# Linear attention and two MLPs: raw weights begun earlier on ScalarE, v loads moved to GpSimd, k's small exponential as its own step

## The chip, the cores and the metric

The kernel runs on one core of a Trainium2 chip. The metric is device time in microseconds (us), the median of several executions; smaller is better. The engines are TensorE (PE; its weight loads are shown as PEld), VectorE (DVE), ScalarE (ACT), GpSimd (POOL) and SyncE (SP, which only issues transfers). An engine works off its own instructions in the order of the program.

## The reference

```python
# q, k, v: (8, 8, 576, 64); q scaled by 8, k by 3.682
q_s = softmax(q, axis=-1); k_s = softmax(k, axis=2)       # over the features; over the sequence
kv = einsum('bhsd,bhse->bhde', k_s, v)
x = einsum('bhsd,bhde->bhse', q_s, kv)                    # -> (4608, 512)
g = x @ w_gate; val = x @ w_val                           # (512, 1536) each
x = (g * sigmoid(g) * val) @ w_out                        # (1536, 512)
h = maximum(maximum(x @ w1, x @ w2), x @ w3)              # (512, 768) each
return h @ w_out2                                         # (768, 512)
```

## The kernel before

The 4608 tokens are nine blocks of 512 (`BLOCKS`): three alone, then three pairs, worked off as six stages. Every fp32 product is made as three products of split factors (`...h` and `...l` are the high and the low part), each a run of six matmuls of 128x512. The pair stages use a scheme with seven products for eight; its unit uses four banks of PSUM (`b0` to `b3`) in turn, and `wino_copy` (L891), `wino_add` (L901), `consume` (L857 is the Silu, L866 the multiply) empty them on ScalarE and VectorE. `wino_hi` (L764) and `wino_lo` (L768) make split weights for it.

Nothing reorders the program afterwards: each engine runs its instructions in the order in which the code issues them. That order has three sources. First the loads, by the table `LOADS`. Then `PROLOGUE`, a table written by hand: each entry is one step, and the program's function `run` issues it. The steps that matter here:

- `load_v` is `first_load_v` (L278): six transfers for each half hf of block 0's v, hf 0 begun by ScalarE, hf 1 by GpSimd. The memsets of `kvhi` and `kvlo` (L2648) stand ahead of all loads on GpSimd.
- `act` is `conv_act` (L602): the raw weights lie as 64-bit numbers; ScalarE makes the upper word (L612) and the lower (L616) into two parts, `dve` is `conv_dve` (L628), which joins them on VectorE and also begins the store and further loads; `hi` (L646) and `lo` (L649) split the joined weight. `act 0` and `act 1` read the first two 512-KB pieces of w_gate, `act 2` the first of w_val.
- `k_exp` (L338, L342) and `q_exp` (L358) are exponentials, `q_sum` and `q_mul` the division of q's softmax, `kv` (L258) the product of k and v on TensorE, `scale` (L406) its division, `qt` (L381) transposes of q, `take` (L388) their copies to SBUF, `x` (L392) the block's x in a bank, `xh` (L484) and `xl` (L487) the two parts of x; `mm` a first product of x and a weight group (L798).
- `silu` (L2611) loads the Silu table ahead of its use.

The index behind a step's name is the half (0 or 1) of block 0 with its four heads, called block 0 and block 1 below and in the steps.

From then on a planner walks through the stages' units and puts work into each engine's gaps by estimated durations; its table of steps for the softmax of k is `k_steps`, a chain for each run (j, hf): j is the token block, hf the half of the heads. There `B` is a step for VectorE or GpSimd, `X` one on ScalarE that counts table loads, `A` one on ScalarE. `k_sub` subtracts k's maximum from the large part (part 0, L195) and the small (part 1, L200), `k_exp` (L206) exponentiates them. Exponentials and the Silu use different tables, so a change between them costs a table load on ScalarE.

The lines the change touches:

Of the kernel before, what the change touches and what calls it, by code (L numbers as in the profile page):

```python
# [11 lines left out]
F32 = mybir.dt.float32  # L12
# [9 lines left out]
def linear_attention_moe_moe_kernel(  # L22
# [170 lines left out]
    def k_sub(t, c, part, eng):  # L193
        if part == 0:
            eng.tensor_tensor(  # L195
                out=t["k"], in0=t["k"],
                in1=c["kb"].unsqueeze(2).to_broadcast([128, HH, R, D]), op=ALU.subtract,
            )
        else:
            eng.tensor_tensor(  # L200
                out=t["kr"][0:SR], in0=t["kr"][0:SR], in1=c["kb"][0:SR], op=ALU.subtract
            )

    def k_exp(t, c, part):
        a = t["kr"][0:SR] if part else t["k"]
        nc.scalar.activation(out=a, in_=a, func=AF.Exp)  # L206
# [69 lines left out]
        )  # L276

    def first_load_v(t, hf):  # L278
        eng = (nc.scalar, nc.gpsimd)[hf]
        for g in range(HP):  # L280
            h0 = hf * HH + 2 * g
            for u in range(2):
                eng.dma_start(
                    out=t["v"][:, 0:R, g, u, 0:D],
                    in_=v[0, h0 + u, 0:SM, :].rearrange("(p r) d -> p r d", r=R),
                )
            eng.dma_start(
                out=t["v"][0:SR, R, g, :, 0:D],
                in_=v[0, h0:h0 + 2, SM:S, :].rearrange("h p d -> p h d"),
            )  # L290
# [932 lines left out]
    def k_steps(runs, n_buf):  # L1223

        steps = []
        loads = [k_loads(kbuf[n % n_buf], *run) for n, run in enumerate(runs)]

        def load(n, part):
            if n < len(runs):
                steps.append(("load", 1.8 if n == 0 else 1.0, ((n, part), loads[n][2:] if part else loads[n][:2])))  # L1230

        load(0, 0)
        load(0, 1)
        for n, (j, hf) in enumerate(runs):
            c, t = {}, kbuf[n % n_buf]
            if j in LATER:
                steps.append(("gate", 0.0, ("later", j)))
            if n_buf == 2:
                load(n + 1, 0)
            steps.append(("loaded", 0.0, (n, 0)))  # L1240
            steps.append(("D=", 1.15, lambda i, c=c, t=t: k_max(t, c, i)))
            steps.append(("loaded", 0.0, (n, 1)))
            steps += [("D", 0.42, lambda c=c, t=t: k_max_rest(t, c)), ("G", 1.4, lambda c=c: k_max_all(c))]
            steps += [("B", (1.22, 0.42)[i], lambda e, c=c, t=t, i=i: k_sub(t, c, i, e)) for i in range(2)]
            steps.append((("X", 1), 1.5, lambda c=c, t=t: (k_exp(t, c, 0), k_exp(t, c, 1))))

            def kv(bank, c=c, t=t):
                for g in range(HP):
                    kv_mm(t, c, g, bank)

            steps += [("wait", KV_WAIT, None), ("P", 1.25, kv)]
            steps += [("D", 1.1, lambda c=c, t=t: kv_scale(t, c)), ("bank", 0.0, None)]
            if n_buf == 1:
                load(n + 1, 0)
            load(n + 1, 1)
            steps += [("gate", 0.0, ("x", j - 2, hf))] * (j > 2) + [
                ("A", 0.6, lambda c=c, j=j, hf=hf: kv_hi(c, j, hf)),
                ("D", 0.4, lambda c=c, j=j, hf=hf: kv_lo(c, j, hf)),
            ]
            steps.append(("open", 0.0, ("kv", j, hf)))  # L1260
        return steps
# [1314 lines left out]
    with tc.manual_schedule():  # L2576
# [17 lines left out]
        def run(name, i, g=None):  # L2594
            t = first[i] if i in (0, 1) else None
            if name == "act":
                conv_act(i, False, i)
            elif name == "dve":
                conv_dve(i, False)
                store_plain(*conv[i])  # L2600
                load_more(i)
            elif name == "hi":
                kind, f = conv[i]
                group_hi(kind, f, (0, kind, f // 2, 0, f % 2), 2 * i)
            elif name == "lo":
                kind, f = conv[i]
                group_lo(kind, f, 2 * i)
            elif name == "load":
                loads(i)
            elif name == "silu":  # L2610
                nc.scalar.activation(out=tops[0], in_=minus_i[:, 0:HP], func=AF.Silu)  # L2611
            elif name == "mm":
                kind, f = conv[i]
                product(("b0", "b2")[i], (0, kind, f // 2, 0, f % 2, 0), "b11", True, True, False)
            elif name.startswith("load_"):
                {"k": first_load_k, "q": first_load_q, "v": first_load_v}[name[5:]](t, i)
            elif name == "xh":
                x_hi(c[i]["px", g], 0, i * HP + g)
            elif name == "xl":
                x_lo(c[i]["px", g], 0, i * HP + g)  # L2620
            else:
                FIRST[name](t, c[i], g)
# [20 lines left out]
        for _ in range(EARLY):  # L2643
            nc.tensor.matmul(
                out=early, lhsT=first[0]["kv"][:, 0], rhs=first[0]["kv"].rearrange("p g n -> p (g n)"), start=True, stop=True
            )
        for a in (*kvhi, *kvlo):
            nc.gpsimd.memset(a.bitcast(F32), 0.0)  # L2648
        for step in LOADS:
            run(*step)  # L2650
        for step in PROLOGUE:
# [9 lines left out]


LOADS = (
    ("load_k", 0), ("load_q", 0), ("load_k", 1), ("load_v", 0), ("load", 1), ("load_q", 1),
    ("load_v", 1), ("load", 6),
)
EARLY = 5
PROLOGUE = (
    ("km", 0), ("plain", 0, 0), ("turn", 0), ("plain", 0, 1), ("top", 0), ("q_max", 0), ("minus", 0, 0),
    ("minus", 0, 1), ("plain", 0, 2), ("minus", 0, 2), ("k_exp", 0, 0), ("k_exp", 0, 1), ("k_exp", 0, 2), ("q_sub", 0),  # L2670
    ("plain", 1, 0), ("plain", 1, 1), ("km", 1), ("q_exp", 0, 0), ("q_exp", 0, 1), ("kv", 0, 0), ("kv", 0, 1),
    ("turn", 1), ("plain", 1, 2), ("q_sum", 0), ("q_mul", 0, 0), ("q_mul", 0, 1), ("qt", 0, 0), ("take", 0, 0),
    ("qt", 0, 1), ("take", 0, 1), ("act", 0), ("scale", 0), ("x", 0, 0), ("x", 0, 1), ("top", 1),
    ("minus", 1, 0), ("minus", 1, 1), ("minus", 1, 2), ("q_max", 1), ("xh", 0, 0), ("xh", 0, 1), ("q_sub", 1), ("k_exp", 1, 0),
    ("k_exp", 1, 1), ("k_exp", 1, 2), ("dve", 0), ("xl", 0, 0), ("xl", 0, 1), ("hi", 0), ("q_exp", 1, 0), ("q_exp", 1, 1),
    ("lo", 0), ("kv", 1, 0), ("kv", 1, 1), ("q_sum", 1), ("act", 1), ("mm", 0), ("silu", 0), ("q_mul", 1, 0), ("q_mul", 1, 1),
    ("scale", 1), ("qt", 1, 0), ("take", 1, 0), ("qt", 1, 1), ("take", 1, 1), ("x", 1, 0), ("x", 1, 1), ("dve", 1), ("hi", 1),
    ("lo", 1), ("act", 2), ("mm", 1), ("xh", 1, 0), ("xh", 1, 1), ("dve", 2), ("hi", 2), ("xl", 1, 0), ("xl", 1, 1), ("lo", 2),
    ("act", 3), ("dve", 3), ("hi", 3), ("lo", 3), ("act", 4), ("act", 5), ("dve", 4), ("dve", 5),
)  # L2680

# [31 lines left out]
```

## Time and profile before

| | us |
|---|---|
| median of 3 runs | 1452.77 (1451.65 to 1453.37) |
| profiled execution | 1452.13, its span 1450.4 |
| PE busy | 1439.6 (99% of the span) |
| DVE busy | 1031.6 (71%) |
| ACT busy | 711.1 (49%) |
| POOL busy | 160.4 (11%) |

The span is the profiled part of an execution; 1.7 us lie around it. A row of the timeline gives start, duration, engine, line, operation, the tiles written and read, and in brackets how long the engine was idle before and what ended that. "xN" is a count of instructions.

### The profile page before, as it was taken

To read this page: it belongs to the slowest core of one execution; us is meant where nothing else is said; L and a number is where in the kernel's file an instruction comes from. 1 tells how busy PE (TensorE), PEld (TensorE's weight loads), DVE (VectorE), ACT (ScalarE), POOL (GpSimd) and SP (SyncE) were. 2 spreads that over 40 slices of the span, in tenths; PEclk is the share of its full clock that TensorE was granted. 3 is DMA by queue.
4 is the path that set the end of the run, shared out by engine and by line. 5 is a ranking of instruction groups with operands and counts; after the bars stand their busy time and mean duration, and the time that the engine had idled before them with its cause. 6 is when DMAs were issued, how large, how long until landed. Compare 5 with 4: busy or idle time off the path is not lost.

```text
span 1450.4 us, 20587 instructions
## 1 busy us (share of the span) xinstructions
PE 1439.6 (99%) x6880; PEld 1178.6 (81%) x6880; DVE 1031.6 (71%) x1815; ACT 711.1 (49%) x1198; POOL 160.4 (11%) x282
## 2 busy tenths in 40 slices
PE   9999999999999999999999999999999999999998
PEld 6887888888888888878878888888888888888887
DVE  7888766968786777788878767667876655577433
ACT  6988654544564435454644463335343532254222
POOL 3111111111222321221021100000000000000000
PEclk9999999999999999999999999999999999999999
DMA  9989588794988898986787587774766676646664
GB/s 273 343 282 363 192 254 245 224 330 142 292 295 299 306 346 290 282 259 197 223 268 241 195 270 229 203 211 153 231 193 199 210 214 195 187 163 223 207 197 155
DMA packets 268456, 347.42 MB, mean 240 GB/s; under 512 B 126304, under 2 KB 152672, under 8 KB 268352
## 3 DMA queue, kind: packets, MB, share of 16 engines
q1 hardware_dynamic: 241904, 263.79, 59.9%
q0 software_dynamic: 23904, 81.61, 14.8%
q8 instruction: 55, 0.90, 0.3%
q10 hardware_dynamic: 2544, 0.72, 0.2%
q14 instruction: 49, 0.40, 0.1%
HBM read 255.59 MB, written 90.44 MB: 239 GB/s over the span
## 4 chain that ended last, share of the span: by engine, by line
PE 93%; DVE 4%; DMA 2%; issue 1%; ACT 1%; SPq 0%; POOL 0%; DVEq 0%; ACTq 0%; POOLq 0%
PE pb L798 61%; PE pacc L819 13%; PE pacc L831 6%; PE pb L831 5%; PE pb L819 3%; PE pkv L258 1%; PE pacc L811 1%; PE px L456 1%; PE px L457 1%; PE px L458 1%; DVE tall L901 1%; DMA twos<-sums_W 1%; PE pacc L798 0%; DMA k_sb<-in_k_dram 0%; DVE wall L768 0%
## 5 line engine op out<-in xcount | busy, mean ns | idle before, releaser
L798 PE MATMUL pb<-t,wall 128*128 128x512 f32 x1116 | 273.5, 390 | 2.0 <-DVE tall L901 2.0
L798 PE MATMUL pb<-b11h,wall 128*128 128x512 f32 x752 | 263.4, 391 | 0.2 <-DVE tall L866 0.2
L798 PE MATMUL pb<-b21h,wall 128*128 128x512 f32 x752 | 262.0, 390 | 0.0
L798 PEld LDWEIGHTS pb<-t,wall 128*128 128x128 f32 x1116 | 208.8, 188 | 47.4 <-issue 1.7
L901 DVE TENSOR_TENSOR tall<-tall,pb 128x512 f32<-128x512 f32 x188 | 128.6, 686 | 125.8 <-PE pb L798 107.3
L798 PEld LDWEIGHTS pb<-b11h,wall 128*128 128x128 f32 x752 | 141.1, 188 | 30.8 <-DVE tall L866 0.6
L798 PEld LDWEIGHTS pb<-b21h,wall 128*128 128x128 f32 x752 | 141.2, 188 | 29.5
L798 PE MATMUL pb<-b21l,wall 128*128 128x512 f32 x376 | 146.6, 390 | 0.7 <-DVE b21l L2028 0.4
L798 PE MATMUL pb<-b11l,wall 128*128 128x512 f32 x376 | 146.5, 390 | 0.0
L891 ACT COPY tall<-pb 128x512 f32<-128x512 f32 x124 | 72.6, 588 | 125.0 <-PE pb L798 118.1
L649 DVE TENSOR_TENSOR wall<-plain,wall 128x512 fp32r<-128x512 f32 x126 | 86.0, 689 | 28.2 <-ACT wall L646 28.0
L646 ACT CAST wall<-plain 128x512 fp32r<-128x512 f32 x126 | 76.0, 617 | 29.5 <-DMA plain<-raw_W 7.3
L866 DVE TENSOR_TENSOR tall<-s,pb 128x512 f32<-128x512 f32 x81 | 55.3, 684 | 47.6 <-PE pb L798 47.4
L819 PE MATMUL pacc<-ow,hhi 128*128 128x512 f32 x288 | 89.1, 390 | 0.0
L819 PE MATMUL pacc<-hhi,ow 128*128 128x512 f32 x264 | 87.8, 395 | 0.0
L798 PE MATMUL pb<-t1h,wall 128*128 128x512 f32 x248 | 86.5, 389 | 0.3 <-DVE tall L901 0.3
L798 PE MATMUL pb<-b22h,wall 128*128 128x512 f32 x248 | 86.6, 390 | 0.0
L798 PEld LDWEIGHTS pb<-b21l,wall 128*128 128x128 f32 x376 | 70.6, 188 | 16.0 <-DVE b21l L2028 0.8
L831 PE MATMUL pacc<-hhi,ow 128*128 128x512 f32 x248 | 82.5, 390 | 0.0
L798 PEld LDWEIGHTS pb<-b11l,wall 128*128 128x128 f32 x376 | 70.6, 188 | 14.1 <-issue 0.2
L831 PE MATMUL pb<-hhi,ow 128*128 128x512 f32 x216 | 68.0, 389 | 0.0
L2002 ACT COPY pb<-pb 128x512 f32<-128x512 f32 x42 | 24.0, 570 | 86.7 <-PE pb L798 86.7
(313 smaller groups left out, 2655.4 us busy)
## 6 DMA issues: line engine op xcount, KB each, us to landing
wall<-wino_W SPq DMA_DIRECT2D x153, 256.0 KB, 3.1
wall<-wino_G SPq DMA_DIRECT2D x102, 256.0 KB, 3.0
wall<-wino_V SPq DMA_DIRECT2D x102, 256.0 KB, 3.1
ow<-owino SPq DMA_DIRECT2D x72, 256.0 KB, 3.4
ow<-parts_P SPq DMA_DIRECT2D x32, 512.0 KB, 5.3
wino_W<-wall POOLq DMA_DIRECT2D x63, 256.0 KB, 4.7
ow<-parts_O SPq DMA_DIRECT2D x56, 256.0 KB, 4.0
wino_G<-wall POOLq DMA_DIRECT2D x42, 256.0 KB, 5.0
```

The lines of the kernel that those rows point to most:

```text
L258: nc.tensor.matmul(out=c["pkv"][u * D:(u + 1) * D, g, :], lhsT=lhsT, rhs=rhs, start=i == 0, stop=i == R,)
L456: nc.tensor.matmul(out=px[:, a:e], lhsT=hi, rhs=qhi, start=True, stop=False)
L457: nc.tensor.matmul(out=px[:, a:e], lhsT=hi, rhs=qlo, start=False, stop=False)
L646: nc.scalar.copy(out=wall[:, i:i + 2, 0], in_=plain[kind, f].rearrange("p (a n) -> p a n", a=2))
L649: eng.tensor_tensor(out=wall[:, i:i + 2, 1], in0=plain[kind, f].rearrange("p (a n) -> p a n", a=2), in1=wall[:, i:i + 2, 0], op=ALU.subtract,)
L798: nc.tensor.matmul(out=banks[bank], lhsT=a, rhs=b, start=start and n == 0, stop=stop and n == 5, skip_group_check=True,)
L819: nc.tensor.matmul(out=banks[bank], lhsT=lhsT, rhs=rhs, start=first and n == 0, stop=last and n == 2)
L831: nc.tensor.matmul(out=banks[bank[e]], lhsT=w[:, a, es], rhs=h[b], start=first and n == 0, stop=last and n == 2, skip_group_check=True,)
L866: eng.tensor_tensor(out=hidden_tile(kind, f, half, tmp), in0=s, in1=a(), op=ALU.mult if kind == "V" else ALU.max)
L891: nc.scalar.copy(out=tall[:, i], in_=banks[bank])
L901: eng.tensor_tensor(out=out_, in0=tall[:, x], in1=banks[bank] if isinstance(bank, str) else tall[:, bank], op=ALU.add)
L2002: nc.scalar.copy(out=banks[bank], in_=banks[other])
```

## The change

`first_load_v` begins only the first three of the twelve v transfers on ScalarE, the other nine on GpSimd. The memsets of `kvhi` and `kvlo` become a step `clear` between GpSimd's first three transfers and the other six. `PROLOGUE` is in another order. In `k_steps`, for j over 4, the two subtractions and the two exponentials are four steps for two and one joint exponential step.

```diff
     def first_load_v(t, hf):
-        eng = (nc.scalar, nc.gpsimd)[hf]
         for g in range(HP):
+            eng = nc.scalar if hf == g == 0 else nc.gpsimd
             h0 = hf * HH + 2 * g
...
-            steps += [("B", (1.22, 0.42)[i], lambda e, c=c, t=t, i=i: k_sub(t, c, i, e)) for i in range(2)]
-            steps.append((("X", 1), 1.5, lambda c=c, t=t: (k_exp(t, c, 0), k_exp(t, c, 1))))
+            sub = lambda e, i, c=c, t=t: k_sub(t, c, i, e)
+            exp = lambda i, c=c, t=t: k_exp(t, c, i)
+            if j > 4:
+                steps += [("B", 1.22, lambda e, f=sub: f(e, 0)), (("X", 1), 1.06, lambda f=exp: f(0))]
+                steps += [("B", 0.42, lambda e, f=sub: f(e, 1)), ("A", 0.42, lambda f=exp: f(1))]
+            else:
+                steps += [("B", (1.22, 0.42)[i], lambda e, f=sub, i=i: f(e, i)) for i in range(2)]
+                steps.append((("X", 1), 1.5, lambda f=exp: (f(0), f(1))))
...
+            elif name == "clear":
+                for a in (*kvhi, *kvlo):
+                    nc.gpsimd.memset(a.bitcast(F32), 0.0)
...
-        for a in (*kvhi, *kvlo):
-            nc.gpsimd.memset(a.bitcast(F32), 0.0)
...
 LOADS = (
-    ("load_k", 0), ("load_q", 0), ("load_k", 1), ("load_v", 0), ("load", 1), ("load_q", 1),
+    ("load_k", 0), ("load_q", 0), ("load_k", 1), ("load_v", 0), ("load", 1), ("load_q", 1), ("clear", 0),
     ("load_v", 1), ("load", 6),
 )
...
-    ("minus", 0, 1), ("plain", 0, 2), ("minus", 0, 2), ("k_exp", 0, 0), ("k_exp", 0, 1), ("k_exp", 0, 2), ("q_sub", 0),
...
+    ("act", 0), ("act", 1), ("turn", 1), ("plain", 1, 2), ("q_sum", 0), ("q_mul", 0, 0), ("q_mul", 0, 1), ("act", 2),
+    ("qt", 0, 0), ("take", 0, 0), ("qt", 0, 1), ("take", 0, 1), ("scale", 0), ("dve", 0), ("x", 0, 0), ("x", 0, 1), ("top", 1),
```

On ScalarE in the prologue, before: from q's first exponential (q_sb) to block 1's (w_81); w_80 and w_82 are parts of k, `shared` the raw weight.

```order
L358 ACTIVATE q_sb<-w_77 128x512 x2
L388 COPY qt<-pt 128x512 x2
L612 ACTIVATE plain<-shared 128x512
L616 ACTIVATE shared<-shared 128x512
L484 CAST b11h<-px 128x512 x2
L338 ACTIVATE w_80<-pk 128x4x128 x2
L342 ACTIVATE w_82<-pk 64x256
L646 CAST wall<-plain 128x2x256
L358 ACTIVATE w_81<-w_79 128x512 x2
```

The same place of the changed program, from block 0's small exponential of k to block 1's exponentials:

```order
L342 ACTIVATE w_82<-pk 64x256
L612 ACTIVATE plain<-shared 128x512
L616 ACTIVATE shared<-shared 128x512
L612 ACTIVATE plain<-shared 128x512
L616 ACTIVATE shared<-shared 128x512
L612 ACTIVATE plain<-shared 128x512
L616 ACTIVATE shared<-shared 128x512
L388 COPY qt<-pt 128x512 x2
L646 CAST wall<-plain 128x2x256
L484 CAST b11h<-px 128x512 x2
L338 ACTIVATE w_80<-pk 128x4x128
L358 ACTIVATE w_81<-w_79 128x512 x2
```

Three conversion pairs for one stand ahead of block 1's exponentials and of the takes (L388); one of k's two L338 and its L342 went behind L358.

On ScalarE near 550 us, before, around the exponentials of run (5, 0): pb is a bank, `s` a Silu's result.

```order
L891 COPY tall<-pb_5208 128x512
L764 CAST wall<-twos 128x256 x3
L857 ACTIVATE s<-tall 128x512
L857 ACTIVATE s<-pb_5194 128x512
L206 ACT_TABLE_LOAD
L206 ACTIVATE k_sb<-k_sb 128x1024
L206 ACTIVATE kr_sb<-kr_sb 64x256
L857 ACT_TABLE_LOAD
L857 ACTIVATE s<-tall 128x512
```

The same place of the changed program:

```order
L891 COPY tall<-pb_5208 128x512
L764 CAST wall<-twos 128x256 x2
L206 ACT_TABLE_LOAD
L206 ACTIVATE k_sb<-k_sb 128x1024
L764 CAST wall<-twos 128x256
L857 ACT_TABLE_LOAD
L857 ACTIVATE s<-tall 128x512
L857 ACTIVATE s<-pb_5194 128x512
L891 COPY tall<-pb_5286 128x512
L206 ACT_TABLE_LOAD
L206 ACTIVATE kr_sb<-kr_sb 64x256
```

The large exponential and two table loads now stand ahead of the Silu that reads bank pb_5194, and the small one stands by itself with a table load of its own.

On ScalarE near 630 us, before, around the exponentials of run (6, 0) (q_sb is q):

```order
L231 ACT_TABLE_LOAD
L231 ACTIVATE q_sb<-q_sb 128x1024
L764 CAST wall<-twos 128x256 x3
L206 ACTIVATE k_sb<-k_sb 128x1024
L206 ACTIVATE kr_sb<-kr_sb 64x256
L879 CAST hhi<-tall 128x512
L891 COPY tall<-pb_6049 128x512
```

The same place of the changed program:

```order
L206 ACT_TABLE_LOAD
L206 ACTIVATE k_sb<-k_sb 128x1024
L857 ACT_TABLE_LOAD
L857 ACTIVATE s<-tall 128x512
L891 COPY tall<-pb_5954 128x512
L891 COPY tall<-pb_5962 128x512
L231 ACT_TABLE_LOAD
L231 ACTIVATE q_sb<-q_sb 128x1024
L206 ACTIVATE kr_sb<-kr_sb 64x256
```

The large exponential of k moved ahead of q's exponential, into the unit before, with two table loads around it; the small one stayed near its place.

## Rows read from the trace of the kernel before

**Rows 1.** The page: busy us, share of the span, instructions.

```profile
PE 1439.6 (99%) x6880; PEld 1178.6 (81%) x6880; DVE 1031.6 (71%) x1815; ACT 711.1 (49%) x1198; POOL 160.4 (11%) x282
```

**Rows 2.** Waits of TensorE, 0 to 34 us: us in total, times, longest.

```profile
PE pt L381 <- ACT w L2611: 1.6, 1, 1.6
```

**Rows 3.** Waits of TensorE, 120 to 1440 us.

```profile
PE pb L798 <- DVE tall L901: 2.3, 4, 1.3
```

**Rows 4.** Timeline of ScalarE in the prologue: start, us, what, idle before and its releaser.

```profile
15.74 1.07 ACT L388 COPY qt<-pt 128x512 f32<-128x512 f32 x2 [3.61 <-PE pt L381]
16.70 0.68 ACT L612 ACTIVATE plain<-shared 128x512 f32<-128x512 f32 x1
...
17.82 1.16 ACT L484 CAST b11h<-px 128x512 fp32r<-128x512 f32 x2
19.26 0.60 ACT L338 ACTIVATE w<-pk 128x512 f32<-128x512 f32 x1 [0.28 <-PE pk L329]
...
21.49 1.15 ACT L358 ACTIVATE w<-w 128x512 f32<-128x512 f32 x2
```

**Rows 5.** Timeline of SyncE's queue: issue of the third and fourth weight pieces.

```profile
10.39 2.51 SPq L599 DMA_DIRECT2D shared<-in_moe_w_val_dram  x2
```

**Rows 6.** DMA issues, 9.9 to 10.6 us: count, KB, us to landing.

```profile
shared<-in_moe_w_val_dram SPq DMA_DIRECT2D x1, 512.0 KB, 9.8
```

**Rows 7.** Timeline of TensorE where the prologue ends.

```profile
30.01 0.39 PE L798 MATMUL pb<-b21h,wall 128*128 128x512 f32 x1
30.69 0.50 PE L798 MATMUL pb<-b21l,wall 128*128 128x512 f32 x1 [0.29 <-DVE b21l L487]
...
33.35 0.39 PE L798 MATMUL pb<-b11h,wall 128*128 128x512 f32 x1
33.58 0.39 PE L798 MATMUL pb<-b11l,wall 128*128 128x512 f32 x1
```

**Rows 8.** Waits of SyncE's queue, 0 to 45 us.

```profile
SPq L269 <- DMA v_sb<-in_v_dram: 2.5, 1, 2.5
SPq L599 <- DMA w<-in_q_dram: 1.8, 1, 1.8
```

**Rows 9.** DMA queues, 12 to 17 us: packets, MB, share (q1 SyncE, q0 GpSimd).

```profile
q1 hardware_dynamic: 1167, 1.16, 84.6%
q0 software_dynamic: 160, 0.33, 24.8%
```

**Rows 10.** DMA queues, 17 to 20.3 us.

```profile
q1 hardware_dynamic: 1152, 1.15, 110.0%
```

**Rows 11.** Timeline of GpSimd, 0 to 12 us.

```profile
3.28 1.56 POOL L2648 MEMSET kvhi<- 128x512 f32 x3
...
6.28 1.69 POOL L283 DMA_DIRECT2D w<-in_v_dram  x2
```

**Rows 12.** Timeline around run (5, 0), VectorE, ScalarE and TensorE.

```profile
549.95 1.06 ACT L764 CAST wall<-twos 128x256 fp32r<-128x256 f32 x3
...
552.79 1.22 DVE L195 TENSOR_TENSOR k_sb<-k_sb,kb 128x1024 f32<-128x1024 f32 x1
...
555.19 0.58 ACT L857 ACTIVATE s<-pb 128x512 f32<-128x512 f32 x1
...
555.78 1.28 ACT L206 ACT_TABLE_LOAD   x1
...
556.07 0.39 PE L798 MATMUL pb<-b11h,wall 128*128 128x512 f32 x1
...
557.08 1.06 ACT L206 ACTIVATE k_sb<-k_sb 128x1024 f32<-128x1024 f32 x1
```

**Rows 13.** Timeline near 636 us, TensorE and ScalarE.

```profile
636.05 0.47 PE L798 MATMUL pb<-t1h,wall 128*128 128x512 f32 x1 [0.30 <-DVE tall L901]
...
638.97 2.99 PE L798 MATMUL pb<-t,wall 128*128 128x512 f32 x12 [1.28 <-DVE tall L901]
...
639.51 0.42 ACT L206 ACTIVATE kr_sb<-kr_sb 64x256 f32<-64x256 f32 x1 [5.43 <-DVE kr_sb L200]
```

**Rows 14.** Busy time of the engines, 620 to 640 us: window, PE, PEld, DVE, ACT, POOL.

```profile
620.00:640.00 20.00, 18.42 (x81) 14.66 (x80) 18.13 (x37) 8.85 (x17) 6.04 (x9) 1.00 0.82 273
```

More of the change, by code (lines that the diff above doesn't have):

```diff
@@ L2669 @@
     ("km", 0), ("plain", 0, 0), ("turn", 0), ("plain", 0, 1), ("top", 0), ("q_max", 0), ("minus", 0, 0),
-    ("minus", 0, 1), ("plain", 0, 2), ("minus", 0, 2), ("k_exp", 0, 0), ("k_exp", 0, 1), ("k_exp", 0, 2), ("q_sub", 0),
[L2671 to L2678, printed above, removed]
+    ("minus", 0, 1), ("plain", 0, 2), ("minus", 0, 2), ("k_exp", 0, 0), ("k_exp", 0, 1), ("q_sub", 0),
+    ("plain", 1, 0), ("plain", 1, 1), ("km", 1), ("q_exp", 0, 0), ("q_exp", 0, 1), ("k_exp", 0, 2), ("kv", 0, 0), ("kv", 0, 1),
+    ("act", 0), ("act", 1), ("turn", 1), ("plain", 1, 2), ("q_sum", 0), ("q_mul", 0, 0), ("q_mul", 0, 1), ("act", 2),
+    ("qt", 0, 0), ("take", 0, 0), ("qt", 0, 1), ("take", 0, 1), ("scale", 0), ("dve", 0), ("x", 0, 0), ("x", 0, 1), ("top", 1),
+    ("hi", 0), ("minus", 1, 0), ("minus", 1, 1), ("minus", 1, 2), ("q_max", 1), ("xh", 0, 0), ("xh", 0, 1), ("q_sub", 1),
+    ("k_exp", 1, 0), ("q_exp", 1, 0), ("q_exp", 1, 1), ("k_exp", 1, 1), ("k_exp", 1, 2), ("xl", 0, 0), ("xl", 0, 1), ("lo", 0),
[3 rows of a table added]
     ("act", 3), ("dve", 3), ("hi", 3), ("lo", 3), ("act", 4), ("act", 5), ("dve", 4), ("dve", 5),
```

3 rows, old and new, of the table PROLOGUE are left out of this document.

## The prediction

> **What bounds the kernel now.** Read the busy shares first [rows 1]: TensorE is busy 99% of the span. A change can therefore only move the few microseconds in which TensorE waits, or add new ones. There are two kinds of them. In the prologue the first products wait for q, k and the weights to be made ready, 1.6 us at one place [rows 2]; after 120 us the largest group is four waits of its unit products for VectorE, 2.3 us in all [rows 3], and two of the four, 0.30 and 1.28 us, stand together near 636 us [rows 13]. The change touches both places, so I work them out one after the other and add.
>
> **The prologue, what sets its end.** The second view to read is ScalarE in order of time [rows 4]. Block 0's takes (the copies of the transposed q) run at 15.74, its x is cast at 17.82, block 1's k is exponentiated from 19.26, block 1's q from 21.49 to 22.64. Call this last end T (21.49 + 1.15). From T the chain runs through VectorE (the sum, the multiply), then the transposes of block 1, its takes, its x and the casts of it, until TensorE runs without a gap. So the prologue costs what T costs, and what lies behind T.
>
> **What moves ahead of T.** (a) The change puts all three first weight conversions, each a pair of instructions, ahead of the takes. In the old order the first pair stands behind the takes: it starts at 16.70 and the cast after it at 17.82, so a pair takes 1.12 us. The third pair reads the third weight piece, the first of w_val. That piece is issued at 10.39 [rows 5] and needs 9.8 us to land [rows 6], so it is there at 20.2. ScalarE runs in order: with landing time L the takes cannot start before L + 1.12, and behind them queue x's cast, k's exponential of block 1 and q's exponential, all that T needs. (b) The exponentials of k's second piece and remainder go behind q's exponential, and the cast of the first weight group goes from there to between the takes and x's cast, the place of a conversion pair that lasted longer. From the takes to k's first exponential are 19.26 - 15.74 = 3.52 us, which don't grow; with 0.60 us for it and 1.15 for q's pair T comes 5.27 us behind the takes, against 22.64 - 15.74 = 6.90 now. That is 1.63 us saved. So T moves by L + 1.12 + 5.27 - 22.64 = L - 16.25.
>
> **What moves behind T.** The third conversion and its VectorE step no longer stand between block 1's takes and the low half of its x. TensorE's two waits there go: the second half block starts at 30.01 and the third weight group's product at 33.35, where twelve matmuls at the 0.23 us from 33.35 to 33.58 would need 2.76; the start at 30.69 shows 0.29 us of the rest as a wait for the low half [rows 7]. That is 0.6 us back. The VectorE step itself now follows the low half; it, the cast and the subtraction behind it take some 0.7 us each, and TensorE has the twelve matmuls to work off meanwhile, so I cost that at nothing; were they late, up to 0.6 us would be lost again. The first product moves ahead of block 1's k-v matmuls, which then run while VectorE makes q's sum and multiply: nothing. The prologue as a whole moves by L - 16.9: neutral if the third piece lands at 16.9, and -2.3 us at best, when the takes start at 15.74 as now (L at or below 14.6).
>
> **When does the third piece land?** For the change: SyncE's queue stops in the first 10 us, 2.5 and 1.8 us at the longest, for landings of a v piece and of q [rows 8]. The program counts completions on eight semaphores in turn, shared by the DMAs of SyncE and ScalarE, so an issue waits for the one eight back. With three DMAs on ScalarE for six these waits shrink, and the weights are issued 2 to 4 us earlier. If an earlier issue were an earlier landing, L would be about 17. Against it: from 12 to 17 us the two queues in use fill the engines, SyncE's 84.6% and GpSimd's v pieces 24.8% [rows 9], and from 17 us SyncE's queue alone has 110% [rows 10] (shares over 100% are overlapping packets). The engines never wait for an issue here; the piece lands 9.8 us after its issue because bytes stand ahead of it. Issuing earlier lengthens that wait. What helps is only v traffic that now comes behind the third piece. GpSimd's clears (six memsets, 3.1 us) used to precede its first v piece, at 6.28 [rows 11]; now three pieces go ahead of the clears and six behind, so the last six start near 3.3 + 2.3 + 3.1 = 8.7, some 2.4 us later (2.3 is three issues, by the pair's 1.69). If all six fell behind the third piece, 24.8% of 5 us and what flowed before 12 us, some 2.6 us, would be saved: L = 17.6. If none, 20.2. In the old trace no v bytes flow after 17 us, so 2.4 us later most are still ahead of 20; about one or two of six fall behind, against which the first weight's store, which its earlier VectorE step releases some 4 us sooner, takes bytes back. I take L = 19.6. Prologue: 19.6 - 16.9 = +2.7 us, with +0.7 and +3.3 as ends.
>
> The Trainium skill ("DMA: Bandwidth & Descriptors", section "Issuing engines are not separate DMA queues") says that DMAs begun on different engines run on the same 16 DMA engines and interleave, and that spreading them saves only issue time. By that rule alone the prologue would take the upper end, +3.3; by the shorter issue waits alone about zero. The rows on the queues' shares side with the rule, and no more than that hangs on it.
>
> **The second part, from 546 us on.** For runs with j over 4 the small exponential of k becomes a step of its own. The orders around the first of them and the third show what follows.
>
> A loss: at (5,0) the big exponential now stands ahead of two Silus, not behind them. VectorE's subtraction that it reads runs from 552.79 for 1.22 us, to 554.01 [rows 12]. Then come, on ScalarE, the exponential (1.06), a cast (a third of 1.06), a table load of 1.28 and the two Silus (0.58 each): 554.05 + 1.06 + 0.35 + 1.28 + 2 x 0.58 = 557.9, a little less where neighbours overlap; I take 557.8. The second Silu frees the bank that TensorE's next unit writes at 556.07. In the old order it starts at 555.19 and is done in time. So +1.75 us of wait, where none is now; nothing hides it, since TensorE's queue is in order. Its lower bound is 0, if the planner's other moves bring the subtraction forward.
>
> A gain: at 639.51 ScalarE had waited 5.43 us for VectorE's small subtraction, and TensorE waits 0.30 and 1.28 us for VectorE's additions there [rows 13], in a stretch in which VectorE is busy 18.13 of 20 us [rows 14]. With the k chain a unit earlier, VectorE has 1.6 us of subtractions less in that unit. I take both waits as gone, -1.5 us; the bound is 0. The small exponential apart from the big one adds eight table loads of 1.28 us; elsewhere ScalarE is half idle (49% busy [rows 1]) and the added loads stand beside copies that have room before their banks are written again, so they cost nothing; were the cover gone, each would cost up to 1.28 us. Together +0.2 us, ends -1.6 and +1.8, and one uncovered load more would make +3.
>
> The Trainium skill ("ScalarE: Activation LUTs", section "What ACT_TABLE_LOAD costs") adds a drain of 1380 ns to each load of 1283 ns. At 555.78 the load took 1.28 us and the exponential began at 557.08, 0.02 us behind it [rows 12], so the drain doesn't show here; with it the stall at 556 would be some 3.1 us and the sum would be +4.3.
>
> **Sum.** +2.7 + 0.2 = +2.9 us. Against the profiled execution's 1452.13 (1450.4 of span and 1.7 around it) that is 1455.0; against the median of the runs, 0.64 higher, 1455.7. I put 1455.3.
>
> **Rivals.**
> 1. *The weights come in time.* v's pieces fall behind the weights, L is 14.6 or less, ScalarE never waits. Then -2.3, and with the two waits near 636 gone and half of the stall at 556 -3 in all: 1449.8; without that stall 1448.9. For it: the freed waits of SyncE. Against it: full DMA engines.
> 2. *Nothing comes earlier and the Silu stalls*, the side further beyond. L is 20.2 or later, +3.3; the Silu waits 1.75, and the waits near 636 stay, because VectorE's work is only regrouped: +5.1, 1457.9. It decides where L passes 19.8 and the 636 waits stay over 1 us.
> 3. *The change does little.* L near 17 and the gain at 636 pays for the loss at 556: within a microsecond of 1452.8. For it: the issues come 2 to 4 us earlier.
>
> **How the numbers follow.** Forecast 45%, its own range 1454.0 to 1456.6; rival 1 20%, rival 2 25%, rival 3 10%. A measurement of this kernel tells about 0.2% (2.9 us) from no change: faster is below 1449.9, slower above 1455.7. Rival 1 gives 17 points of faster and 3 of same; rival 3 is same; of the forecast two thirds is same (30) and a third slower (15); of rival 2 22 slower, 3 same. So 17, 46 and 37. The range runs from 1449.5, which keeps a part of rival 1, to 1458.0, the end of rival 2; some 2 in 10 stays outside.
>
> **What would show it.** In the changed profile's prologue: ScalarE idle ahead of the third conversion, released by the DMA of the w_val piece, the takes near 20.7 for 15.74, q's exponential ending near 26, TensorE's first gapless run beginning 2 to 3 us later. Takes at 16 mean rival 1. At 556 us TensorE waiting for a Silu of ScalarE, some 1.8 us; near 636 no wait for VectorE over 0.4. I am wrong if the third piece lands before 17, or if the second part has a wait at a place that I hold covered.

## The result and the profile after

| | before | after |
|---|---|---|
| median, us | 1452.47 (1451.65 to 1453.37, 6 runs) | 1464.24 (1463.34 to 1465.99, 6 runs) |
| span of the profiled execution, us | 1450.4 | 1461.6 |
| PE busy, us | 1439.6 | 1443.7 |
| ACT busy, us | 711.1 | 721.4 |

The changed kernel is slower by a ratio of 1.0081 (95% interval 1.0068 to 1.0094), 11.8 us. I had forecast 1455.3, and a range up to 1458.0: the side was right, the size was not, and the time lies outside.

Both kernels run the same 6880 matmul records on TensorE, so the start of the n-th record in one trace can be set against the n-th in the other. Where both stand at the same place of the program, TensorE is later after the change by:

| place (time before) | later by, us |
|---|---|
| the third weight group's product, 33 to 37 us | 6.2 |
| 60 us, and without change up to 470 us | 7.6 |
| 546 us | 7.5 |
| 557 us, behind the unit with run (5, 0) | 9.4 |
| 718 us | 10.7 |
| 760 us | 9.5 |
| 860 us and the end | 11.0 |

The step back from 10.7 to 9.5 belongs to the trace of before: it waits for a VectorE step near 737 us and is then some 1 us later against every one of the other thirteen traces below (0.8 to 1.3 us). The table therefore shows the second part about that much too small. TensorE's timeline of the kernel before at that place:

```profile
737.46 0.50 PE L798 MATMUL pb<-b21l,wall 128*128 128x512 f32 x1 [0.38 <-DVE b21l L2028]
```

So there are three losses: the prologue, a smaller one behind it, and the second part. First the prologue. ScalarE's timeline of the kernel after (start, us, engine, line, operation, idle before and its releaser; compare [rows 4]):

```profile
13.32 0.68 ACT L612 ACTIVATE plain<-shared 128x512 f32<-128x512 f32 x1 [0.70 <-DMA shared<-in_moe_w_gate_dram]
...
19.16 0.67 ACT L612 ACTIVATE plain<-shared 128x512 f32<-128x512 f32 x1 [4.59 <-DMA shared<-in_moe_w_gate_dram]
...
20.66 0.66 ACT L612 ACTIVATE plain<-shared 128x512 f32<-128x512 f32 x1 [0.27 <-DMA shared<-in_moe_w_val_dram]
...
21.76 1.05 ACT L388 COPY qt<-pt 128x512 f32<-128x512 f32 x2
...
28.34 1.14 ACT L358 ACTIVATE w<-w 128x512 f32<-128x512 f32 x2
```

ScalarE idles 4.59 us for the second weight piece and waits again for the third, which lands at 20.64; the takes follow 1.10 us behind its conversion's start at 20.66. T is 28.34 + 1.14 = 29.48, for 22.64 before. The DMA issue row of the third piece, issued at 8.28 us, of the kernel after ([rows 6] is that of before; the last number is us to landing):

```profile
shared<-in_moe_w_val_dram SPq DMA_DIRECT2D x1, 512.0 KB, 12.4
```

The DMA queues from 12 to 17 us of the kernel after, as in [rows 9]:

```profile
q1 hardware_dynamic: 970, 0.96, 70.2%
q0 software_dynamic: 200, 0.52, 40.3%
```

It was issued 2.1 us earlier than before and took 2.6 us longer: GpSimd's v pieces moved 0.52 MB in these 5 us, for 0.33 before.

The waits of TensorE from 0 to 60 us of the kernel after (us in total, times, longest):

```profile
PE px L392 <- ACT qt L388: 5.1, 1, 5.1
...
PE pb L798 <- ACT wall L646: 0.4, 1, 0.4
```

TensorE's timeline behind the first of them:

```profile
22.38 3.78 PE L392 MATMUL px<-qt,w 128*128 128x512 f32 x4 [5.09 <-ACT qt L388]
25.96 3.29 PE L329 MATMUL pk<-w 128*128 128x256 f32 x12
```

The four records of x take 3.78 us; before the change they took 1.98. The windows say why. Columns are the window, its length, busy time (and instructions) of PE, PEld, DVE, ACT and POOL, then the granted clock, the DMA share and GB/s:

```profile
16.00:20.00 4.00, 1.30 (x10) 0.85 (x8) 3.86 (x7) 0.83 (x2) 0.59 (x1) 1.00 1.07 292
...
21.00:22.00 1.00, 0.00 (x0) 0.00 (x0) 0.00 (x0) 1.00 (x3) 0.00 (x0) 0.50 1.13 362
22.00:26.00 4.00, 3.62 (x5) 1.54 (x6) 0.69 (x1) 1.92 (x4) 0.00 (x0) 0.50 1.07 381
...
28.00:32.00 4.00, 4.00 (x54) 2.93 (x52) 2.50 (x6) 3.71 (x7) 0.00 (x0) 1.00 0.00 0
```

While TensorE waited, its granted clock fell to 0.50, the 1.2 GHz level, and it stayed there through x and block 1's k until 27.6 us.

In the second part, the waits of TensorE from 60 us to the end, of the kernel after ([rows 3] has before's largest group):

```profile
PE pkv L258 <- DVE tall L901: 2.1, 1, 2.1
PE pb L798 <- ACT s L857: 2.0, 2, 1.7
PE pb L798 <- DVE tall L901: 1.1, 4, 0.5
PE pb L798 <- DVE s L901: 0.9, 1, 0.9
```

The waits for VectorE's additions fell from 2.3 to 1.1 us, as hoped, but three new ones came. The largest for ScalarE is the Silu at run (5, 0) (timeline of the kernel after, ScalarE and TensorE, answering to [rows 12]):

```profile
561.51 1.06 ACT L206 ACTIVATE k_sb<-k_sb 128x1024 f32<-128x1024 f32 x1 [2.08 <-DVE k_sb L195]
...
562.88 1.28 ACT L857 ACT_TABLE_LOAD   x1
...
564.71 0.58 ACT L857 ACTIVATE s<-pb 128x512 f32<-128x512 f32 x1
...
565.34 0.50 PE L798 MATMUL pb<-b11h,wall 128*128 128x512 f32 x1 [1.65 <-ACT s L857]
```

The wait of the k-v matmuls of run (6, 0) has a longer chain (timeline of the kernel after, ScalarE, VectorE and TensorE, where [rows 13] were):

```profile
631.76 1.28 ACT L206 ACT_TABLE_LOAD   x1
...
635.12 1.28 ACT L857 ACT_TABLE_LOAD   x1
...
638.17 1.28 ACT L231 ACT_TABLE_LOAD   x1
...
640.74 0.60 ACT L879 CAST hhi<-tall 128x512 fp32r<-128x512 f32 x1
...
641.37 0.69 DVE L882 TENSOR_TENSOR hlo<-tall,hhi 128x512 fp32r<-128x512 f32 x1 [4.19 <-ACT hhi L879]
...
643.32 0.69 PE L258 MATMUL pkv<-v_sb,k_sb 128*64 128x66 f32 x16 [2.09 <-DVE tall L901]
```

Three table loads in 8 us (to k's exponential, back to Silu, to q's exponential), with the exponentials and copies between them, put off ScalarE's cast of a hidden tile. VectorE stands 4.19 us at the subtraction that reads it, and behind that subtraction is the addition that frees the bank which the k-v matmuls need.

### The profile page after: what moved, and what is told of

It is laid out like the page before. It is cut to its first block, busy times and chain, and to the rows that moved or that the text cites. A ratio compares the mean times of both kernels' runs of the same rounds, so it can differ in the third digit from the quotient of the medians.

```text
span 1461.6 us, 20612 instructions
## 1 busy us (share of the span) xinstructions
PE 1443.7 (99%) x6880; PEld 1180.0 (81%) x6880; DVE 1030.7 (71%) x1815; ACT 721.4 (49%) x1206; POOL 161.8 (11%) x285
## 4 chain that ended last, share of the span: by engine, by line
PE 91%; DVE 3%; ACT 2%; DMA 2%; issue 1%; SPq 0%; ACTq 0%; DVEq 0%
PE pb L798 59%; PE pacc L819 13%; PE pacc L831 6%; PE pb L831 5%; PE pb L819 3%; PE pkv L258 1%; DMA shared<-in_moe_w_val_dram 1%; PE pacc L811 1%; DVE tall L901 1%; PE pacc L798 1%; PE px L456 1%; PE px L457 1%; PE px L458 1%; DMA w<-in_q_dram 0%; ACT L857 0%
## 5 line engine op out<-in xcount | busy, mean ns | idle before, releaser
L649 DVE TENSOR_TENSOR wall<-plain,wall 128x512 fp32r<-128x512 f32 x126 | 85.8, 688 | 28.3 <-ACT wall L646 27.6
L646 ACT CAST wall<-plain 128x512 fp32r<-128x512 f32 x126 | 76.3, 619 | 29.0 <-DMA plain<-raw_W 8.7
```

The source lines that it names most:

```text
L646: nc.scalar.copy(out=wall[:, i:i + 2, 0], in_=plain[kind, f].rearrange("p (a n) -> p a n", a=2))
L649: eng.tensor_tensor(out=wall[:, i:i + 2, 1], in0=plain[kind, f].rearrange("p (a n) -> p a n", a=2), in1=wall[:, i:i + 2, 0], op=ALU.subtract,)
```

## The experiments

The theory after the result: the prologue loses by ScalarE standing in front of weight pieces that land no earlier, and by the clock that falls in TensorE's wait; the second part loses by table loads and order on ScalarE; the two parts add. Each kernel was timed beside runs of the kernel before on the same chip, whose medians were 1452.22, 1452.56 and 1452.45 us; "over before" refers to the one beside it. "At 60 us" below is how much later TensorE stands at that place than in the trace of before; kernels with an unchanged prologue scatter there by 0.3 to 0.9 us.

**The two parts alone.** pro_only has the changed loads and prologue and the old k_steps, k_only the reverse.

> The changed prologue and v loads alone, k_steps as before. Theory (the prologue's loss is the third weight piece, landing near 20.6 us, plus a drop of TensorE's granted clock in the wait for it): 7.6 us over the kernel before, all of it in place by 60 us of the span, and TensorE's order and times afterwards shifted by a constant. Rival (the two parts interact, the later prologue upsets the order in the second part): clearly less than 7.6, with the rest appearing only when both are there.

> The split of k's exponentials alone, prologue and loads as before. Theory (the parts add): 3.4 us over the kernel before, of which 1.8 to 1.9 us at the unit that starts at 556 us, where TensorE waits for a Silu. Rival (the second part's waits come from the late prologue): within 0.5 us of before.

pro_only against the changed kernel; k_only is the kernel before with this hunk the other way round:

```diff
-            if j > 4:
-                steps += [("B", 1.22, lambda e, f=sub: f(e, 0)), (("X", 1), 1.06, lambda f=exp: f(0))]
-                steps += [("B", 0.42, lambda e, f=sub: f(e, 1)), ("A", 0.42, lambda f=exp: f(1))]
```

pro_only 1458.60 us (ratio 1.0044, 1.0029 to 1.0059), 6.4 over before, and 7.2 at 60 us; k_only 1457.69 (1.0036, 1.0024 to 1.0048), 5.5 over. Together 11.9, and the changed kernel is 11.8 over: the parts add, as far as intervals of some 2 us on each can tell. In its trace pro_only keeps 6.7 of the 7.2 us up to 718 us and ends at 5.6, for the wait near 737 us that only before has. The changed kernel loses 5.0 us more than pro_only does between 60 us and the end (+3.4 against -1.6).

The second part is dearer than the 3.4 us that I read from the shifts. Some of that is the wait near 737 us; in k_only some is the clock. Near 636 us its TensorE waits 2.09 us for a bank, as the changed kernel does near 643 (2.09 too), and in the profiled execution of k_only the granted clock falls to 0.50 behind that wait, in that of the changed kernel it doesn't. TensorE's timeline and a window of k_only (the granted clock is the third figure from the end):

```profile
638.10 2.90 PE L798 MATMUL pb<-t,wall 128*128 128x512 f32 x6
```

```profile
639.00:640.00 1.00, 1.00 (x4) 0.71 (x4) 1.00 (x3) 0.00 (x0) 0.00 (x0) 0.50 0.99 307
```

From the k-v matmuls to the first product behind these six, TensorE needs 4.33 us in k_only and 2.80 in the changed kernel. Of k_only's six executions the two with a mean granted clock of 1.000 took 1456.3 and 1456.7 us, the four with 0.999 took 1457.7 to 1459.1.

TensorE's waits from 60 us on in k_only show the same three places as the changed kernel:

```profile
PE pkv L258 <- DVE tall L901: 2.1, 1, 2.1
PE pb L798 <- ACT s L857: 2.0, 2, 1.7
PE pb L798 <- DVE s L901: 0.9, 1, 0.9
```

**The clock.** Eleven matmuls that nobody reads keep TensorE busy while it would wait; nothing else changes.

> pro_only with 11 matmuls of 128x256 whose result nobody reads, on TensorE between block 0's transposes and its x, so that TensorE is busy for some 4.7 us of its wait for the takes. Theory (the wait lets the granted clock fall to 1.2 GHz, which costs 2.4 us on x, k and the row behind it): the clock stays at 2.4 GHz from 21 to 28 us, and the run is 2.0 to 2.6 us faster than pro_only. Rival (the slow matmuls there come from something else, such as the transfers that fill SBUF at the time): they stay slow and the time is that of pro_only, or later by the added work.

> The changed kernel with 11 matmuls of 128x256 whose result nobody reads, on TensorE between block 0's transposes and its x, as in pro_warm. Theory (in the wait for the takes the granted clock falls, and that costs 2.1 to 2.5 us of the changed kernel's loss): 1461.7 to 1462.3, against 1464.2 for the changed kernel, and 2.4 GHz throughout the prologue. Rival (the clock's fall costs nothing that shows in the end, since the conversions up to 50 us bind behind it): within 0.7 us of the changed kernel.

```diff
+            elif name == "warm":
+                spare = ps.tile([128, 128 * HP], F32, tag="b3", name="spare")
+                for _ in range(g):
+                    nc.tensor.matmul(out=spare, lhsT=ident, rhs=first[0]["kv"].rearrange("p g n -> p (g n)"), start=True, stop=True)
...
-    ... ("scale", 0), ("dve", 0), ("x", 0, 0), ...
+    ... ("scale", 0), ("warm", 0, 11), ("dve", 0), ("x", 0, 0), ...
```

ScalarE's timeline of pro_warm:

```profile
21.94 1.04 ACT L388 COPY qt<-pt 128x512 f32<-128x512 f32 x2
...
25.93 1.14 ACT L358 ACTIVATE w<-w 128x512 f32<-128x512 f32 x2
```

The same window of pro_only and then of pro_warm, with the granted clock third from the end:

```profile
23.00:24.00 1.00, 1.00 (x2) 0.48 (x3) 0.00 (x0) 0.78 (x2) 0.00 (x0) 0.50 1.04 371
```

```profile
23.00:24.00 1.00, 1.00 (x4) 0.43 (x3) 0.00 (x0) 0.79 (x2) 0.00 (x0) 1.00 1.09 386
```

The takes start as late as in pro_only (22.21 there), the clock stays at 1.00, and T comes 5.13 us behind the takes for 6.95. TensorE reaches the product at which ScalarE's fourth cast is awaited at 43.21 for 45.30, and stands 5.2 us late at 60 us for 7.2. The whole time shows less than the 2.0 to 2.6 us that were expected: 1457.79 us (1455.74 to 1459.95), 0.8 under pro_only, less than the spread. after_warm measured 1462.31 (ratio 1.0068, 1.0054 to 1.0082), 1.9 under the changed kernel, with intervals that overlap. In its profiled execution, the slowest of its four, the third piece landed only at 22.4 and the clock fell to 0.50 near 644 us, behind the wait of the k-v matmuls.

The mechanism is shown by the clock and by the distance from takes to T. Its worth in the whole time was 0.8 and 1.9 us in these runs, and neither is clear of the noise.

**v's queues.** The order on ScalarE as changed with the old loads, and the new loads with the old order.

> The changed PROLOGUE table with the old v loads, old place of the clears and k_steps as before. Theory (what costs is the order on ScalarE, whatever queue v takes): the third weight piece lands near 20.2 us, the takes start near 21.4, the granted clock falls as in pro_only, and the time is within 1.5 us of pro_only, 1457 to 1459. Rival (v behind GpSimd's clears holds the weights up): 2 us or more faster than pro_only.

> The new v loads and clears with the old PROLOGUE table and k_steps as before. Theory: SyncE's queue now issues q and weights earlier and they share the engines with block 1's k, which lands 1.5 us later (11.6 for 10.1); TensorE has that k's matmuls ahead of block 0's transposes, so the takes start near 17 for 15.74 and the whole comes out 0.5 to 1.5 us over the kernel before. Rival (as the prediction costed it, v's move acts through the third weight piece alone): within 0.3 us of before.

v_only against the kernel before; pro_oldv is pro_only with this the other way round:

```diff
-        eng = (nc.scalar, nc.gpsimd)[hf]
+            eng = nc.scalar if hf == g == 0 else nc.gpsimd
...
-    ... ("load_q", 1),
+    ... ("load_q", 1), ("clear", 0),
```

pro_oldv: 1458.72 us (1.0045, 1.0028 to 1.0062), within 0.2 us of pro_only. ScalarE in pro_oldv:

```profile
20.40 0.66 ACT L612 ACTIVATE plain<-shared 128x512 f32<-128x512 f32 x1 [0.29 <-DMA shared<-in_moe_w_val_dram]
...
21.51 1.05 ACT L388 COPY qt<-pt 128x512 f32<-128x512 f32 x2
```

Over the profiled executions the third piece is there at 20.2 to 21.0 with the old queues and at 20.6 to 21.1 with the new ones (once at 22.4). The loss is the order's. v_only: 1453.32 us (1.0009, 1.0000 to 1.0019), 0.8 us over, at the edge of the noise; its profiled execution took 1454.52. TensorE's timeline of v_only shows where it comes from:

```profile
11.77 1.98 PE L308 MATMUL pk<-w,w 128*128 128x512 f32 x4 [1.03 <-DMA w<-in_k_dram]
...
16.21 1.09 PE L381 MATMUL pt<-w,q_sb 128*128 128x128 f32 x8
```

Block 1's k, issued at 2.64 as before (2.63), landed at 11.7 for 10.1, and its matmuls stand ahead of block 0's transposes, which began at 15.04 before. The bytes of v that moved up to 10.1 us are about the same (0.58 MB for 0.56); SyncE's queue issues other pieces earlier, among them the first weight piece (4.92 us for 8.01) and a piece of q (6.11 for 8.44). Which of them holds k up was not separated. I had costed v's move through the third weight piece alone.

**Which conversion.** The second and third put back (new loads), then the third alone (old loads), and the second and third with the third VectorE step ahead of the low half of x again (old loads).

> pro_only with the second and third weight conversion back where they were (behind block 1's exponentials, and behind its takes). Theory (the loss is ScalarE standing in front of the third piece): takes of block 0 at 16 to 17.5 us, no drop of the clock, q's exponential of block 1 ends near 22 to 23, and the whole is within 1.5 us of the kernel before, between 1451 and 1454. Rival (the v loads on GpSimd or the other moves of the prologue carry the loss): still 4 us or more over before.

> pro_oldv with the third conversion alone in its old place (behind block 1's takes) and the third VectorE step ahead of the low half of x again; the second conversion stays ahead of the takes. Theory (the takes come 1.1 us behind the landing of the last piece that ScalarE converts ahead of them, and T 5.3 us behind the takes while the clock holds): second piece at 18.9, takes near 20.0, T near 25.3, and with the clock held 2 to 3 us over before, 1454.5 to 1455.6. Rival (TensorE's wait of some 4 us lets the clock fall here too): takes near 20.0 as well, but T near 27.5 and 4.5 to 5.5 over before.

> The old v loads and k_steps as before; the changed PROLOGUE with the second and third conversion in their old places and the third VectorE step ahead of the low half of x again. What is left of the change: the first conversion ahead of the takes, the exponentials of k behind that of q, the first product ahead of block 1's k-v matmuls. Theory (these moves save the 1.6 us ahead of T, and ScalarE's conversions behind T move with it): takes at 15.7 to 15.9 us, q's exponential of block 1 ends near 21, 1 to 2 us faster than before, 1450.2 to 1451.2. Rival (the conversions up to 43 us bound the prologue, not T): within 0.5 us of before.

pro_acts_back against pro_only, and behind it what acts_back_oldv has besides, on the old loads; act2_back has the last two of the four edits and, of the first, `act 2` alone:

```diff
-    ("act", 0), ("act", 1), ("turn", 1), ... ("q_mul", 0, 1), ("act", 2),
+    ("act", 0), ("turn", 1), ... ("q_mul", 0, 1),
-    ("k_exp", 1, 1), ("k_exp", 1, 2), ("xl", 0, 0), ...
+    ("k_exp", 1, 1), ("k_exp", 1, 2), ("act", 1), ("xl", 0, 0), ...
-    ("dve", 1), ("hi", 1), ("lo", 1),
+    ("dve", 1), ("hi", 1), ("lo", 1), ("act", 2),
...
-    ("xl", 1, 0), ("xl", 1, 1), ("dve", 2), ("hi", 2), ("lo", 2),
+    ("dve", 2), ("hi", 2), ("xl", 1, 0), ("xl", 1, 1), ("lo", 2),
```

pro_acts_back: 1452.23 us (0.9999, 0.9990 to 1.0009), no loss left. It gains 0.6 us up to 37 us and stands 1.2 us late at 60. The wait of TensorE for ScalarE from 0 to 60 us in pro_acts_back:

```profile
PE pb L798 <- ACT wall L646: 0.9, 1, 0.9
```

ScalarE's timeline in pro_acts_back, at the cast of the third weight group:

```profile
31.25 0.62 ACT L646 CAST wall<-plain 128x512 fp32r<-128x512 f32 x1 [1.47 <-DVE plain L628]
```

The third VectorE step behind the low half leaves ScalarE idle for 1.47 us in a chain of conversions that has no room until 43 us. The loads are not the reason: pro_oldv, on the old ones with that step behind, goes from 5.9 us late at 37 to 7.3 at 60, and act2_back, on the old ones with the step ahead, from 5.3 to 5.2. acts_back_oldv, where that step is ahead again, has no wait for L646 (one of 0.6 us for a low part, L649, at 22.3 us), stands 0.5 us early at 60 us, and is the only kernel here whose interval lies under 1, if barely: 1451.13 us (0.9990, 0.9981 to 0.9999). It was expected at 1450.2 to 1451.2; T fell by 1.0 us only, because the first weight piece landed at 15.0 in its profiled execution and q's subtraction also came later.

act2_back: 1456.07 us (1.0024, 1.0013 to 1.0034). ScalarE's timeline of act2_back:

```profile
19.00 0.67 ACT L612 ACTIVATE plain<-shared 128x512 f32<-128x512 f32 x1 [3.24 <-DMA shared<-in_moe_w_gate_dram]
...
20.11 1.06 ACT L388 COPY qt<-pt 128x512 f32<-128x512 f32 x2
...
26.75 1.14 ACT L358 ACTIVATE w<-w 128x512 f32<-128x512 f32 x2
```

A window of act2_back:

```profile
22.00:23.00 1.00, 1.00 (x2) 0.42 (x2) 0.00 (x0) 0.15 (x1) 0.00 (x0) 0.50 1.09 387
```

The takes come where the sum put them (20.0), and the clock falls in a wait of 4.0 us too: T is 27.9, the rival's number. At 3.6 us over before the whole is between the two that were expected. Seven kernels with the new order in one table, from such rows (T - takes was worked out as 5.27 for a held clock):

| kernel | conversion of the last piece awaited starts | takes | T | T - takes | clock behind the takes |
|---|---|---|---|---|---|
| after | 20.66 | 21.76 | 29.48 | 7.72 | 0.50 |
| pro_only | 21.10 | 22.21 | 29.16 | 6.95 | 0.50 |
| pro_oldv | 20.40 | 21.51 | 29.17 | 7.66 | 0.50 |
| act2_back | 19.00 | 20.11 | 27.89 | 7.78 | 0.50 |
| pro_warm | 20.81 | 21.94 | 27.07 | 5.13 | 1.00 |
| after_warm | 22.40 | 23.50 | 28.65 | 5.15 | 1.00 |
| acts_back_oldv | 15.03 | 16.17 | 21.66 | 5.49 | 1.00 |

**The Silu table.** One more step to make the best kernel better.

> acts_back_oldv with the load of the Silu table moved behind the fourth conversion, where ScalarE idled 0.76 us; the load reads and writes a tile on which block 1's transposes wait. Theory (the transposes then start when q's multiply is done, and ScalarE has the load in idle time): the first product after the transposes starts 0.3 to 0.9 us earlier, 0.2 to 0.8 us faster than acts_back_oldv, 1450.3 to 1450.9. Rival (VectorE's scale binds there): as acts_back_oldv, 1451.1.

```diff
-    ("mm", 0), ("kv", 1, 0), ("kv", 1, 1), ("q_sum", 1), ("silu", 0), ...
+    ("mm", 0), ("kv", 1, 0), ("kv", 1, 1), ("q_sum", 1), ...
-    ("act", 3), ("dve", 3), ("hi", 3), ...
+    ("act", 3), ("dve", 3), ("silu", 0), ("hi", 3), ...
```

1451.21 us (0.9994, 0.9985 to 1.0003), as acts_back_oldv. At 37 us TensorE is 0.4 us ahead of acts_back_oldv, but it got that at 22.3 us, by the wait for a low part (L649) that acts_back_oldv has there and this run hasn't, ahead of the transposes: the first weight piece landed at 14.7 for 15.0. The moved load brought nothing at the transposes, and at 38.7 to 41.8 us TensorE lost 0.6, with a wait for the low part of a later weight group (silu_late, waits of TensorE from 0 to 60 us):

```profile
PE pb L798 <- DVE wall L649: 0.2, 1, 0.2
```

So the table load had less room in the chain of conversions than its idle 0.76 us suggested.

**Which run of k.** The split for block 5 alone, and for blocks from 6 on.

> k_only with the split for j equal to 5 only. Theory (splitting block 5's runs shows the Silu wait of 1.8 us at 556 us and pulls run (6, 0) forward, whose k-v matmuls then wait 2.2 us for a bank near 636 us in place of the two waits of 1.9 us there): both places as in k_only, 2.5 to 4 us over before, 1455 to 1456.5. Rival (the wait of the k-v matmuls comes from the split of block 6's own runs): the two old waits of 0.46 and 1.46 us near 636 are back and the time is 1.8 to 2.5 over before.

> k_only with the split for j over 5 in place of j over 4. Theory (each of the second part's waits belongs to one run of k): the wait of 1.8 us for the Silu at 556 us is gone, the time is 1.8 to 3 us under k_only, 1454.7 to 1456. Rival (the split gives the planner another order whose loss comes anyhow, wherever it starts): within 1 us of k_only.

k_run5 against k_only; k_from6 has `j > 5` there:

```diff
-            if j > 4:
+            if j == 5:
```

k_run5: 1454.57 us (1.0014, 1.0004 to 1.0023), 2.1 over before; k_from6: 1454.74 (1.0015, 1.0006 to 1.0025), 2.2 over. k_run5 has the Silu wait of 1.7 us. At 636 us it has neither the wait of the k-v matmuls nor the two old ones, so both of what I expected was wrong there: splitting block 5 alone brings the gain that I forecast (TensorE is 2.1 us late at 620 us and 0.8 at 660). ScalarE there, in k_run5:

```profile
628.84 1.28 ACT L206 ACT_TABLE_LOAD   x1
630.14 1.06 ACT L206 ACTIVATE k_sb<-k_sb 128x1024 f32<-128x1024 f32 x1
631.10 0.40 ACT L206 ACTIVATE kr_sb<-kr_sb 64x256 f32<-64x256 f32 x1
...
632.18 1.06 ACT L231 ACTIVATE q_sb<-q_sb 128x1024 f32<-128x1024 f32 x1
```

Run (6, 0) comes a unit earlier, undivided, and shares one table load with q. In k_from6 the Silu wait at 556 is gone, as expected; the old waits near 636 are still there, and smaller ones come later (waits of TensorE from 60 us on):

```profile
PE pb L798 <- DVE tall L901: 1.8, 3, 1.3
PE pb L831 <- DVE hlo L882: 0.7, 1, 0.7
...
PE px L456 <- ACT s L860: 0.5, 1, 0.5
```

So the 2.1 us of the k-v matmuls need both: block 5's split, which pulls run (6, 0) forward, and block 6's, which parts its exponentials and adds the loads.

## Why the prediction was wrong, point by point

**The landing of the third piece.** I took 19.6 us; it was 20.6. Full engines gave nothing for an earlier issue, and GpSimd's v pieces were not behind it but beside it (0.52 MB for 0.33 from 12 to 17 us). This is a term mis-sized by 1.0 us. The rule of the Trainium skill that I weighed there ("DMA: Bandwidth & Descriptors", "Issuing engines are not separate DMA queues"), that DMAs begun on different engines share the same 16 DMA engines and spreading them saves only issue time, was the better guide. The traces agree with it: pro_oldv lands the piece at 20.4 on the old queues, the changed kernel at 20.6 on the new ones. The upper end of the prologue, +3.3, was the sum for that case.

**Takes and T.** Right: takes 1.10 to 1.14 us behind the start of the last conversion in the seven kernels of the table, and T 5.1 to 5.5 behind the takes in the three with a held clock, for 5.27 worked out.

**The clock was left out.** This is the step of the prologue that failed; the second part has one of its own, below. I let every duration of TensorE stand as the trace of before has it, at full clock, while my own sum made it wait about 4 us for the takes. The rows show 0.50 behind waits of 4.0 to 5.2 us, and 1.7 to 2.5 us more from the takes to T. Here 7.72 - 5.27 = 2.45. The Trainium skill ("TensorE: Matmul & The Clock Gate", "What's actually happening") states that half rate is the default and activity releases it. The traces agree in that the clock fell to 0.50 in each of these four waits. A fall belonged in the sum as soon as the sum had a wait of TensorE in it.

With both, the prologue is 20.64 - 16.9 + 2.45 = 6.2, as measured at 37 us.

**Behind T.** The 0.6 us came (6.8 at the second half block, 6.2 at the third group). But I called the third VectorE step behind the low half free, with a loss of at most 0.6. It cost 1.4 us at 45 and 49 us: I looked at the next product only, not at ScalarE's chain of conversions behind it, which had no room. pro_acts_back against acts_back_oldv shows it: 1.2 us late and 0.5 early at 60 us; so does, on the same old loads, pro_oldv against act2_back.

**The second part.** I had +0.2; it measured 3.4 us against the trace of before, 5.0 against that of pro_only, and 5.5 alone, with the clock's fall in k_only. The Silu term was right: +1.75 forecast, 1.82 by the starts. The gain near 636 was right as far as the old waits go; they are gone. What failed is the sentence that the added table loads cost nothing. Three loads in 8 us delayed a cast, a subtraction and an addition in turn, and the k-v matmuls wait 2.1 us. k_run5, with one load there, has no such wait; since its order on ScalarE differs as well, the share of the loads alone is not shown. I had looked at how busy ScalarE is on average (49%) and at copies with room, not at the one cast behind the loads on which VectorE's queue hangs. The wait of 0.9 us for VectorE near 781 us comes with the split of block 5 (k_run5 has it); what leads to it was not traced further.

**The rivals.** The second, with no earlier landing and the Silu's stall, was nearest: it gave 1457.9 and lacked the clock, the conversions' 1.4 us and the new wait. It was not right for its own reasons throughout: it kept the old waits near 636 us, and they went.

## What to carry to other kernels

Before a conversion is moved ahead of other work on an in-order engine, look at when its data lands on a saturated queue: an earlier issue buys nothing there, and everything behind the instruction waits. A sum that makes TensorE wait some microseconds must price what runs behind the wait at the lower clock, as long as no row of the same kernel shows the clock held through such a wait. An engine that is half idle on average still carries chains: of each added table load ask which instruction stands next behind it, and who waits for that.

## What the runs showed of the hardware that was not expected

The granted clock didn't fall for the same wait every time. Before the change TensorE waits 1.57 us near 24 us and its clock stays at 1.00; in the profiled execution of v_only the same wait (1.6 us) is followed by a clock of 0.50 from 28 to 30 us, which is one microsecond of its 2.1 late at 60. Behind the k-v matmuls' wait of 2.1 us near 640 us it fell in k_only and in after_warm, and held in the changed kernel. In all four kernels with a wait of 4.0 us or more it was at 0.50 before the wait was over. When exactly it falls, these runs don't settle.

The transfer of one 512-KB weight piece took 9.8 us from issue to landing when issued at 10.39 and 12.4 us when issued at 8.28: with the engines full, the landing moved by 0.4 us while the issue moved by 2.1.
